# A Fourier mixing layer and a gated dense layer in seven-product blocks: the fifth block's second row taken from the first row's partial, and two blocks of dense columns by turns

## The chip, the cores and the metric

One core of one Trainium2 chip runs the whole kernel. The metric is the device time in microseconds (us) from the launch to the end, taken as the median of several executions. A profile of one further execution gives the times of single instructions.

## What is computed

`x` is 2048 tokens by 640 features. The result mixes a two-dimensional Fourier transform of `x` (real part) with a two-layer network, by a gate per token:

```python
a = x @ dft_hid_re.T                      # 2048 x 640
b = x @ dft_hid_im.T
fnet = dft_seq_re @ a - dft_seq_im @ b    # 2048 x 640, real part only
h = x @ w1 + b1                           # 2048 x 1728
dense = mish(h) @ w2                      # mish(h) = h * tanh(softplus(h))
g = sigmoid((x * gate_w).sum(-1))
out = g * fnet + (1 - g) * dense
```

## The kernel before

Four stages follow one another: `seq` (the transform along the 2048 tokens, real and imaginary part), `hid` (the transform along the 640 features), the dense first product with mish, and `out` (the dense second product, to which the gated Fourier part is added at the end). All numbers are float32. Each operand is split into a high and a low part (`split`: ScalarE copies with rounding, VectorE subtracts), and each product of blocks is three matmuls of 128x128 by 128x512 (`mm3`): high by high, high by low, low by high.

**Seven products.** `seq`, `hid` and `out` are written as problems (`sq[0..3]`, `hd[0..1]`, `ou[0..1]`). Each has five row blocks of 128 output features, of which four are computed as a two by two block product with seven instead of eight multiplications, and two column tiles `t1`, `t2` of 512. A problem has three parts. `first` runs the product with the block a11. `second` runs over the operands a22, a21, s2 and s1 (called "22", "21", "s2", "s1"). `third` runs "12", s3 and s4. The sums s1 = a21 + a22, s2 = s1 - a11, s3 = a11 - a21, s4 = a12 - a22 + s3 are formed by VectorE (`sums`) and split (`c_split`). Results grow in the eight accumulation banks, under the names `a`, `b`, `c`, `p4`, and `d1`, `d2` for the fifth row block, which is computed plainly: `d1` (column tile `t1`) gets a product with a11 in `first` and one with a12 in `third`; `d2` (tile `t2`) gets one with a22 and one with a21, both in `second`. `copy_out` copies banks to SBUF with ScalarE, `preload` copies SBUF values into a bank with ScalarE so that matmuls go on adding to them, `done` copies a finished bank out, `give` finishes the rows that s3 completes. In `ou[0]` `done` and `give` multiply by the gate and add the Fourier part, on VectorE. In `ou[1]` (`early`) the Fourier part is added to the partial values beforehand. Problems `sq[1]`, `sq[2]`, `hd[1]` and `ou[1]` run their `first` well ahead: its three banks are stored to DRAM (`aside`) and loaded again before `second`. `rest` adds to `out` the last 192 rows of the contraction.

**The dense first product** (`dense_first(tp)`, once for each half of the tokens) goes over six pairs of column blocks `fp`, with eight steps for each: p1, p5, d2, p6, p3, p7, p2, p4 (54 matmuls). Bank `a` is used by p1, then copied out by ScalarE (`snap`), added to by p6, copied out again, added to by p7, added to `KEEP["p5"]` by VectorE, and added to by p4. Bank `b` is used by p5, copied out, and added to by p3. So a step of the matmuls waits for a copy or an addition of an earlier step. `sums_of` (eight additions of VectorE) and `make` (splits of x) are attached to given steps by the lists at the end of the program.

**What sets the order.** The program is written out by hand, step by step. In the loop over steps, at step i: loads are issued up to `AHEAD` = 9 steps past those being prepared, when more SBUF slots (`FS`, 20) are free than `spare` reserves; the preparations of step i + 7 (6 in the dense stage) are issued; then the matmuls of step i; then stores that are due; then `post` of step i and the events `at(i, ...)`; then jobs (weights of a later stage: `low`, `top`, `w1`), as long as VectorE's planned clock is behind TensorE's. `store` queues a store three steps late. Each engine works its instructions in the order in which they are issued, and so does SyncE with nearly all loads and stores: a load of a scratch tensor waits there for the store of it, and a load into a slot for the last reader of the slot.

Of the kernel before, what the change touches and what calls it, by code (L numbers as in the profile page):

```python
# [13 lines left out]
P = 128  # L14
# [31 lines left out]
def fnet_mish_gate(ctx: ExitStack, tc: tile.TileContext, xn, xt, c_re, c_im, wd_re, wd_im,  # L46
# [134 lines left out]
    def b_sums(f, g):  # L181

        t = FS.get()
        tt(f[:, A2], f[:, B2], f[:, A2], OP.subtract)
        tt(f[:, B2], g[:, B2], f[:, B2], OP.subtract)
# [107 lines left out]
    class Problem:  # L293
# [8 lines left out]
        def first(self, new=False):  # L302
            st, kh = self.st, self.st.kh
            pa, pd = ("ax", "dx") if self.aside else ("a", "d1")
            for k in range(kh):
                key = ("c", st.kind, len(steps))
                raw = [(key, self.moving(self.t1, k))]
                start, last = not len(steps), k == kh - 1

                def prep(k=k, key=key):  # L310
                    if new:
                        f = RAW.pop(("xa", k))
                        top(st, k, f[:, A2], xd(k))
# [24 lines left out]
                if last:  # L338
                    takes[len(steps)] = 3 if self.aside else 2
                step(raw, [prep], mms, post if last else None)  # L340


        def second(self):
# [4 lines left out]
            def sums(k, raws):  # L348
                a22, a21, a11 = (RAW.pop(r[0]) for r in raws)
                s1 = FS.get()  # L350
                tt(s1, a21, a22, OP.add)
                tt(a11, s1, a11, OP.subtract)
                own.update({("22", k): a22, ("21", k): a21, ("s1", k): s1, ("s2", k): a11})
# [3 lines left out]
                "21": lambda k: [("d2", blocks(st.XA[k], 2 * P, 1))],  # L357
# [3 lines left out]
            opens = {("22", "p4"), ("22", "d2"), ("s1", "b")}  # L361
# [5 lines left out]
            def post(p, k):  # L367
# [4 lines left out]
                elif p == "21":  # L372
                    self.done("d2", 4, t2)
# [7 lines left out]
                    if self.aside:  # L381
                        d = [RAW.pop(("part", 2))]
                        if self.early:
                            y = YT.pop((4, t1))
                            tt(d[0], d[0], y, OP.add)
                            FS.put(y)
                        preload("d1", d)
                        FS.put(*d)
# [16 lines left out]
            if st.kind == "out":  # L405
# [4 lines left out]
                rest(t2, [("e", 2, True), ("e", 3, True), ("p4", 0, True), ("p4", 1, True), ("d2", 4, True)], e_post)  # L410
            for p, k in in_turn(kh, ("22", "21", "s2", "s1"), ("22", "21", "s2", "s1"), ("22", "21", "s2", "s1")):
# [7 lines left out]
                def mms(p=p, k=k, key=key):  # L419
# [4 lines left out]
                    if self.end and (p, k) in ends:  # L424
                        W.put(st.XA[k])
                        if k == kh - 1:
                            W.put(*[w for w in st.XT2 if w])
                preps.append(lambda p=p, k=k, key=key: c_split(key, own.pop((p, k))))
                step(raw, preps, mms, lambda p=p, k=k: post(p, k))
                if k == kh - 1:  # L430
                    takes[i] = (p == "21" or p == "s1" and 2) if self.early else 1 if p == "21" else 2
                    if self.early and p != "s1":
                        takes[i - 4] = 2
                        if p == "21":
                            self.y_load(i - 4, t2, 4)
                            self.y_load(i - 4, t1, 0, 1, 4)
                        else:
                            self.y_load(i - 4, *{"22": (t2, 0, 1), "s2": (t1, 2, 3)}[p])
                if (p, k) == ("21", kh - 1):
                    done = i  # L440
            if self.out:
                for t in (t1, t2):
                    at(n - 2, lambda t=t: QT.update({t: fs_load(qsc[t])}))
                self.y_load(done - 5, t2, 4)
            ends = {("s1", k) for k in range(kh)}
            if self.aside:
                for j in range(3):
                        at(n - 6 if j < 2 else done - 6, lambda j=j: RAW.update({("part", j): fs_load(self.aside[j])}))
# [3 lines left out]
        def third(self, over=False):  # L452
# [3 lines left out]
            def sums(k, raws):  # L456
                a12, a11, a21, a22 = (RAW.pop(r[0]) for r in raws)
                tt(a11, a11, a21, OP.subtract)
                FS.put(a21)
                tt(a22, a22, a11, OP.subtract)  # L460
                tt(a22, a12, a22, OP.subtract)
                own.update({("12", k): a12, ("s3", k): a11, ("s4", k): a22})
# [3 lines left out]
                "s3": lambda k: [("a", blocks(st.XT13[k], 2 * P, 2))],  # L466
# [13 lines left out]
            def post(p, k):  # L480
# [4 lines left out]
                elif p == "s3":  # L485
# [4 lines left out]
                    free_banks("a")  # L490
                elif p == "12":
# [5 lines left out]
            for p, k in in_turn(kh, ("12", "s3", "s4"), ("12", "s3", "s4"), ("s3", "12", "s4")):  # L497
# [14 lines left out]
                def mms(p=p, k=k, key=key):  # L512
# [4 lines left out]
                    op_done(key)  # L517
                    if self.end and p == "s4":
# [3 lines left out]
                if k == kh - 1 and p != "s3":  # L522
                    takes[i] = 3 if p == "12" else 2
                if self.out and k == kh - 1:
                    self.y_load(i - (4 if p == "s3" else 2), *{"s3": (t2, 0, 1, 2, 3), "12": (t1, 0, 1, 4), "s4": (t1, 2, 3)}[p])
# [5 lines left out]
        def done(self, name, d, t):  # L531

            for j, ps in enumerate(PS.pop(name)):
# [4 lines left out]
                elif self.early and name == "d2":  # L538
                    y = YT.pop((d, t))
                    tt(f, ps, y, OP.add)  # L540
                    FS.put(y)
# [192 lines left out]
    def dense_first(tp, end, ops):  # L734
# [32 lines left out]
        def sub(fp, ops, then=()):  # L767

            def mms():
                a, b, c = W1[fp]  # L770
                for bank, name, blk, start, stop in ops:
                    if start:
                        H[bank] = psum.get()
                    for k in range(2):
                        mm3(H[bank], *blk(a, b, c, k), *X[name, k, tp], start and k == 0, stop and k == 1)
                for bank, name, w, start, stop in then:
                    if start:
                        H[bank] = psum.get()
                    mm3(H[bank], *part((a, b)[w], 4 * P, 5 * P), *X[name, 0, tp], start, stop)
# [31 lines left out]
        for fp in range(FP):  # L811
            fa, fb = fp, fp + FP
            over = fp == FP - 1

            def free(*names, over=over):
# [3 lines left out]
            def p1_post(free=free):  # L819
                snap("p1", "a")  # L820
                free("a11")

            def p5_post(free=free):
                snap("p5", "b")
                free("s1")

            def p6_post(free=free):
                snap("u2", "a")
                free("s2")

            def p3_post(free=free, fb=fb):
                o = add("b", KEEP.pop("u2"))
                pop("b")
# [3 lines left out]
            def p7_post(free=free):  # L837
                add("a", KEEP["p5"])
                free("s3")

            def p2_post(free=free, fa=fa, fb=fb):
                c11, c22 = add("c", KEEP.pop("p1")), add("d", KEEP.pop("p5"))
                pop("c")
                pop("d")
# [5 lines left out]
            def p4_post(free=free, fa=fa, fp=fp):  # L850
                ps = H.pop("a")
# [10 lines left out]

            step([], [lambda fp=fp: need(("w1", fp))], sub(fp, [("a", "a11", at_cols(0, 0), True, True)]), p1_post)
            step([], [], sub(fp, [("b", "s1", at_cols(2, 0), True, True)]), p5_post)
            step([], [], sub(fp, [], [("d", "d2", 1, True, True)]))
            step([], [], sub(fp, [("a", "s2", t2_at(fp), False, True)]), p6_post)
            step([], [], sub(fp, [("b", "s4", at_cols(1, 2 * P), False, False)], [("b", "d1", 1, False, True)]), p3_post)
            step([], [], sub(fp, [("a", "s3", at_cols(2, 2 * P), False, True)]), p7_post)
            step([], [], sub(fp, [("c", "a12", at_cols(0, 2 * P), True, False)], [("c", "d1", 0, False, True)]), p2_post)
            step([], [], sub(fp, [("a", "a22", at_cols(1, 0), False, False)], [("a", "d2", 0, False, True)]), p4_post)  # L870
# [129 lines left out]
    for tp in range(2):  # L1000
# [132 lines left out]
```

## Time and profile before

| | |
|---|---|
| runs | 885.35, 886.82, 889.29 us (median 886.82) |
| profiled execution, first to last instruction (span) | 882.2 us |
| matmuls (TensorE) | 3780, busy 864.0 us (98% of the span) |
| VectorE | 1262 instructions, busy 724.2 us (82%) |
| ScalarE | 909 instructions, busy 477.5 us (54%) |
| DMA | 217.32 MB, 246 GB/s in the mean |

For the profiled execution only its span is given, 882.2 us; what lies around it is taken as the difference to the median of the runs, 4.6 us. In the profile's lines PE is TensorE, DVE is VectorE, ACT is ScalarE and SPq is SyncE's queue. Tile names are without buffer numbers: `ps` is a bank, `f` and `fx` are SBUF slots, `rh`, `rl` the high and low part of a moving operand, `wh`, `wl` those of a stationary one. "x3" at the end of a line counts instructions, and a bracket tells how long the engine had been idle and what ended that.

### The profile page before, as it was taken

What the parts mean: (1) busy time and instruction counts of PE and PEld (TensorE: products, weight loads), DVE (VectorE), ACT (ScalarE), POOL (GpSimd) and SP (SyncE); (2) the same over time, 40 slices, a digit from 0 to 9 for tenths busy, and PEclk for the clock granted to TensorE, in tenths of its full rate; (3) what the DMA queues carried; (4) which work ended last, traced back from release to release, by engine and by line L of the source; (5) the groups of instructions that cost most, each with busy time, mean ns of one, the idle gap of its engine ahead of it and who ended that gap; (6) DMA issues with size and microseconds to landing.
All of it is one profiled execution on the core that took longest, in us unless ns stands there. A gap on an engine that the chain in (4) does not pass through costs nothing.

```text
span 882.2 us, 12203 instructions
## 1 busy us (share of the span) xinstructions
PE 864.0 (98%) x3780; PEld 710.4 (81%) x3780; DVE 724.2 (82%) x1262; ACT 477.5 (54%) x909; POOL 0.2 (0%) x4
## 2 busy tenths in 40 slices
PE   8999999999999999999999999899899999999998
PEld 6888888888888888888888888687688788888886
DVE  5999987899799668998997987663875889798994
ACT  6756545454565545647665667543644656442442
POOL 0000000000000000000000000000000000000000
PEclk9999999999999999999999999999999999999999
DMA  9975759596889664768767795489676777394952
GB/s 323 328 236 175 245 185 324 164 312 235 302 275 351 202 221 156 259 226 283 265 236 273 247 316 178 138 308 367 204 256 214 268 260 240 133 330 142 367 203 107
DMA packets 119392, 217.32 MB, mean 246 GB/s; under 512 B 13600, under 2 KB 16032, under 8 KB 119328
## 3 DMA queue, kind: packets, MB, share of 16 engines
q1 hardware_dynamic: 119184, 216.43, 71.6%
q8 instruction: 29, 0.48, 0.2%
q14 instruction: 35, 0.29, 0.1%
q10 hardware_dynamic: 144, 0.13, 0.0%
HBM read 170.11 MB, written 46.40 MB: 245 GB/s over the span
## 4 chain that ended last, share of the span: by engine, by line
PE 93%; DVE 3%; ACT 1%; DMA 1%; issue 1%; SPq 0%; DVEq 0%; ACTq 0%
PE ps L89 93%; DVE f L77 1%; DVE wl L77 1%; ACT wh L80 1%; DMA y<-f 1%; DVE rl L77 0%; DMA f<-in_xn_dram 0%; ACT f L671 0%; DMA act<-f 0%; DVE fx L77 0%; ACT f L80 0%; ACT rh L80 0%; SPq L1031 0%; SPq L1051 0%; DVE f L477 0%
## 5 line engine op out<-in xcount | busy, mean ns | idle before, releaser
L89 PE MATMUL ps<-rh,wh 128*128 128x512 f32 x1067 | 415.7, 390 | 7.4 <-ACT f L80 3.4
L89 PE MATMUL ps<-rh,wl 128*128 128x512 f32 x1053 | 409.4, 389 | 0.0
L89 PE MATMUL ps<-rl,wh 128*128 128x512 f32 x1052 | 409.1, 389 | 0.0
L80 ACT ACTIVATE rh<-f 128x512 fp32r<-128x512 f32 x413 | 243.7, 624 | 158.3 <-DVE f L77 103.9
L77 DVE TENSOR_TENSOR rl<-f,rh 128x512 fp32r<-128x512 f32 x411 | 267.0, 685 | 47.7 <-ACT rh L80 47.0
L89 PEld LDWEIGHTS ps<-rh,wh 128*128 128x128 f32 x1067 | 200.4, 188 | 52.7 <-ACT f L80 5.0
L89 PEld LDWEIGHTS ps<-rh,wl 128*128 128x128 f32 x1053 | 197.7, 188 | 40.9
L89 PEld LDWEIGHTS ps<-rl,wh 128*128 128x128 f32 x1052 | 197.4, 188 | 40.9 <-DVE rl L77 0.2
L77 DVE TENSOR_TENSOR f<-f,f 128x512 f32<-128x512 f32 x303 | 207.0, 689 | 19.2 <-DMA u<-f 6.3
L80 ACT ACTIVATE f<-ps 128x512 f32<-128x512 f32 (+1 forms) x146 | 84.9, 593 | 92.7 <-PE ps L89 74.7
L80 ACT ACTIVATE wh<-f 128x512 fp32r<-128x512 f32 (+2 forms) x158 | 68.9, 475 | 49.4 <-DVE f L77 40.4
L77 DVE TENSOR_TENSOR f<-ps,f 128x512 f32<-128x512 f32 x90 | 59.0, 685 | 35.1 <-PE ps L89 35.1
L77 DVE TENSOR_TENSOR wl<-f,wh 128x512 fp32r<-128x512 f32 (+2 forms) x157 | 73.8, 502 | 16.2 <-ACT wh L80 16.0
L89 PE MATMUL ps<-wh,wh 128*128 128x512 f32 x201 | 79.3, 395 | 5.4 <-ACT f L80 2.8
L89 PE MATMUL ps<-wl,wh 128*128 128x512 f32 x196 | 77.0, 393 | 0.0
L89 PE MATMUL ps<-wh,wl 128*128 128x512 f32 x195 | 76.6, 393 | 0.0
L77 DVE TENSOR_TENSOR wl<-fx,wh 128x640 fp32r<-128x640 f32 (+3 forms) x82 | 43.7, 554 | 11.6 <-ACT wh L80 11.6
L671 ACT ACTIVATE f<-f,b1s 128x512 f32<-128x512 f32 x36 | 25.9, 721 | 49.2 <-DVE f L77 49.2
L89 PEld LDWEIGHTS ps<-wh,wh 128*128 128x128 f32 x201 | 38.0, 189 | 15.4 <-ACT f L80 4.2
L80 ACT ACTIVATE wh<-fx 128x128 fp32r<-128x128 f32 (+5 forms) x83 | 40.6, 514 | 10.5 <-DMA fx<-in_xn_dram 3.5
L89 PEld LDWEIGHTS ps<-wh,wl 128*128 128x128 f32 x195 | 37.0, 190 | 7.8
L89 PEld LDWEIGHTS ps<-wl,wh 128*128 128x128 f32 x196 | 37.1, 189 | 7.5
(43 smaller groups left out, 177.3 us busy)
## 6 DMA issues: line engine op xcount, KB each, us to landing
f<-in_c_re_dram SPq DMA_DIRECT2D x128, 256.0 KB, 4.2
f<-in_c_im_dram SPq DMA_DIRECT2D x128, 256.0 KB, 4.1
f<-act SPq DMA_DIRECT2D x84, 256.0 KB, 5.2
f<-u SPq DMA_DIRECT2D x80, 256.0 KB, 4.6
f<-in_xt_dram SPq DMA_DIRECT2D x64, 256.0 KB, 4.6
act<-f SPq DMA_DIRECT2D x54, 256.0 KB, 4.5
u<-f SPq DMA_DIRECT2D x40, 256.0 KB, 3.5
y<-f SPq DMA_DIRECT2D x40, 256.0 KB, 4.5
```

What stands on the lines that cost most here:

```text
L77: nc.vector.tensor_tensor(o, a, b, op=op)
L80: nc.scalar.activation(o, a, AF.Copy, scale=scale)
L89: nc.tensor.matmul(ps, a, b, start=start, stop=stop, skip_group_check=True)
L671: nc.scalar.activation(o[rows], src[rows], AF.Mish, bias=b1s[rows, f:f + 1])
```

## The change

**Fifth block.** With s3 taken as a21 - a11, the second column tile of the fifth row block is (five x a11) + (five x s3) + (its lower half x a22). So `d2` now begins as a copy of the partial value of `d1` after `first`; the "21" step of `second`, with its split of a21, goes; and "s3" of `third` gets one more product, into `d2`. Where `first` was run ahead, the partial is loaded six steps before `second`, and `preload` copies it into `d2`'s bank at the end of the step just before `second` (`d_ready`); in `ou[1]` VectorE first adds the Fourier part. `d2` is finished after s3, in `third`. It holds a bank from `first` or the beginning of `second` to there. The stationary blocks `XA` are given back in `third`. A problem has one step fewer for each k.

**Dense stage.** `dense_first` takes two pairs of column blocks by turns: p1 of the one, p1 of the other, p5 of the one, and so on. Banks have the names (a..d, 0) and (a..d, 1), eight in all. The lists that attach sums and splits to steps have new step numbers.

The counts in the built program: matmuls 3780 as before, VectorE's instructions 54 fewer, ScalarE's 41 fewer (54 splits gone; 8 preloads, 4 copies out and one copy more), the DMAs the same in number.

```diff
@@ Problem.first
                     else:
-                        KEEP["p1"] = copy_out("a", True)
+                        KEEP["p1"], KEEP["d"] = copy_out("a", True), copy_out("d1", True)
+                        preload("d2", KEEP["d"])
+                        FS.put(*KEEP.pop("d"))
@@ Problem.second
-                s1 = FS.get()
-                tt(s1, a21, a22, OP.add)
-                tt(a11, s1, a11, OP.subtract)
+                tt(a21, a21, a22, OP.add)
+                tt(a11, a21, a11, OP.subtract)
...
-                "21": lambda k: [("d2", blocks(st.XA[k], 2 * P, 1))],
...
+            def d_ready():
+                d = KEEP["d"] = RAW.pop(("part", 2))
+                if self.early:
+                    y = YT.pop((4, t2))
+                    tt(y, y, d, OP.add)
+                    preload("d2", [y])
+                    FS.put(y)
+                else:
+                    preload("d2", [d])
...
-            for p, k in in_turn(kh, ("22", "21", "s2", "s1"), ("22", "21", "s2", "s1"), ("22", "21", "s2", "s1")):
+            for p, k in in_turn(kh, ("22", "s2", "s1"), ("22", "s2", "s1"), ("22", "s2", "s1")):
...
+                at(n - 1, d_ready)
                 at(n, a_ready)
@@ Problem.third
-                tt(a11, a11, a21, OP.subtract)
-                FS.put(a21)
-                tt(a22, a22, a11, OP.subtract)
+                tt(a21, a21, a11, OP.subtract)
+                FS.put(a11)
+                tt(a22, a22, a21, OP.add)
...
-                "s3": lambda k: [("a", blocks(st.XT13[k], 2 * P, 2))],
+                "s3": lambda k: [("a", blocks(st.XT13[k], 2 * P, 2)), ("d2", blocks(st.XA[k], 2 * P, 1))],
...
                     free_banks("a")
+                    self.done("d2", 4, t2)
@@ dense_first
-        for fp in range(FP):
-            fa, fb = fp, fp + FP
+        def one(fp):
+            fa, fb, j = fp, fp + FP, fp % 2
...
+        for f0 in range(0, FP, 2):
+            for pair in zip(one(f0), one(f0 + 1)):
+                for st in pair:
+                    step(*st)
@@ program
-    dense_first(0, False, [("k0", n0 + 2), ("k1", n0 + 2), ("s1", n0 + 3), ("s2", n0 + 4), ("s4", n0 + 6), ("s3", n0 + 7)])
+    dense_first(0, False, [("k0", n0 + 2), ("k1", n0 + 2), ("s1", n0 + 3), ("s2", n0 + 6), ("s4", n0 + 8), ("s3", n0 + 10)])
     n0 = len(steps)
-    dense_first(1, True, [("a11", n0 - 1), ("k0", n0), ("k1", n0 + 1), ("s1", n0 + 1), ("d2", n0 + 2), ("s2", n0 + 3),
-                          ("s4", n0 + 4), ("d1", n0 + 4), ("s3", n0 + 5), ("a12", n0 + 6), ("a22", n0 + 7)])
+    dense_first(1, True, [("a11", n0 - 2), ("k0", n0 - 1), ("k1", n0), ("s1", n0 + 2), ("s2", n0 + 5), ("d2", n0 + 6),
+                          ("s4", n0 + 7), ("d1", n0 + 8), ("s3", n0 + 9), ("a12", n0 + 11), ("a22", n0 + 13)])
```

More of the change, by code (lines that the diff above doesn't have):

```diff
@@ L338, in first @@
                 if last:
-                    takes[len(steps)] = 3 if self.aside else 2
+                    takes[len(steps)] = 3
                 step(raw, [prep], mms, post if last else None)
@@ L381, in post @@
                     if self.aside:
-                        d = [RAW.pop(("part", 2))]
+                        d = KEEP.pop("d")
                         if self.early:
                             y = YT.pop((4, t1))
-                            tt(d[0], d[0], y, OP.add)
+                            tt(d, d, y, OP.add)
                             FS.put(y)
-                        preload("d1", d)
-                        FS.put(*d)
+                        preload("d1", [d])
+                        FS.put(d)
                 elif p == "s2":
@@ L409, in second @@
                     self.y_load(n - 4, t2, 2, 3)
-                rest(t2, [("e", 2, True), ("e", 3, True), ("p4", 0, True), ("p4", 1, True), ("d2", 4, True)], e_post)
-            for p, k in in_turn(kh, ("22", "21", "s2", "s1"), ("22", "21", "s2", "s1"), ("22", "21", "s2", "s1")):
+                rest(t2, [("e", 2, True), ("e", 3, True), ("p4", 0, True), ("p4", 1, True), ("d2", 4, False)], e_post)
+            for p, k in in_turn(kh, ("22", "s2", "s1"), ("22", "s2", "s1"), ("22", "s2", "s1")):
                 i, key = len(steps), ("c", st.kind, len(steps))
@@ L423, in mms @@
                     op_done(key)
[L424 to L427, printed above, removed]
+                    if self.end and p == "s2" and k == kh - 1:
+                        W.put(*[w for w in st.XT2 if w])
                 preps.append(lambda p=p, k=k, key=key: c_split(key, own.pop((p, k))))
@@ L430, in second @@
                 if k == kh - 1:
-                    takes[i] = (p == "21" or p == "s1" and 2) if self.early else 1 if p == "21" else 2
+                    takes[i] = (p == "s1" and 2) if self.early else 2
                     if self.early and p != "s1":
                         takes[i - 4] = 2
-                        if p == "21":
-                            self.y_load(i - 4, t2, 4)
+                        if p == "22":
+                            self.y_load(i - 4, t2, 0, 1)
                             self.y_load(i - 4, t1, 0, 1, 4)
                         else:
-                            self.y_load(i - 4, *{"22": (t2, 0, 1), "s2": (t1, 2, 3)}[p])
-                if (p, k) == ("21", kh - 1):
-                    done = i
+                            self.y_load(i - 4, t1, 2, 3)
             if self.out:
@@ L443, in second @@
                     at(n - 2, lambda t=t: QT.update({t: fs_load(qsc[t])}))
-                self.y_load(done - 5, t2, 4)
-            ends = {("s1", k) for k in range(kh)}
             if self.aside:
                 for j in range(3):
-                        at(n - 6 if j < 2 else done - 6, lambda j=j: RAW.update({("part", j): fs_load(self.aside[j])}))
+                    at(n - 6, lambda j=j: RAW.update({("part", j): fs_load(self.aside[j])}))
+                if self.early:
+                    self.y_load(n - 6, t2, 4)
+                at(n - 1, d_ready)
                 at(n, a_ready)
@@ L517, in mms @@
                     op_done(key)
+                    if self.end and p == "s3":
+                        W.put(st.XA[k])
                     if self.end and p == "s4":
@@ L521, in third @@
                 step(raw, preps, mms, lambda p=p, k=k: post(p, k))
-                if k == kh - 1 and p != "s3":
-                    takes[i] = 3 if p == "12" else 2
+                if k == kh - 1:
+                    takes[i] = {"12": 3, "s3": 1, "s4": 2}[p]
                 if self.out and k == kh - 1:
-                    self.y_load(i - (4 if p == "s3" else 2), *{"s3": (t2, 0, 1, 2, 3), "12": (t1, 0, 1, 4), "s4": (t1, 2, 3)}[p])
+                    self.y_load(i - (4 if p == "s3" else 2), *{"s3": (t2, 0, 1, 2, 3, 4), "12": (t1, 0, 1, 4), "s4": (t1, 2, 3)}[p])
                     if p == "s4":
@@ L537, in done @@
                     self.add_y(d + j, t, f)
[L538 to L541, printed above, removed]
                 else:
@@ L772, in mms @@
                     if start:
-                        H[bank] = psum.get()
+                        H[bank, fp % 2] = psum.get()
                     for k in range(2):
-                        mm3(H[bank], *blk(a, b, c, k), *X[name, k, tp], start and k == 0, stop and k == 1)
+                        mm3(H[bank, fp % 2], *blk(a, b, c, k), *X[name, k, tp], start and k == 0, stop and k == 1)
                 for bank, name, w, start, stop in then:
                     if start:
-                        H[bank] = psum.get()
-                    mm3(H[bank], *part((a, b)[w], 4 * P, 5 * P), *X[name, 0, tp], start, stop)
+                        H[bank, fp % 2] = psum.get()
+                    mm3(H[bank, fp % 2], *part((a, b)[w], 4 * P, 5 * P), *X[name, 0, tp], start, stop)
             return mms
@@ L848, in p2_post, with p4_post @@
                 free("a12", "d1")
-            def p4_post(free=free, fa=fa, fp=fp):
-                ps = H.pop("a")
+            def p4_post():
+                ps = H.pop(("a", j))
                 def last():
@@ L861, in p4_post @@
                         W.put(T2B[fp // KD])
[L863 to L870, printed above, removed]
+            return [
+                ([], [lambda: need(("w1", fp))], sub(fp, [("a", "a11", at_cols(0, 0), True, True)]), p1_post),
+                ([], [], sub(fp, [("b", "s1", at_cols(2, 0), True, True)]), p5_post),
+                ([], [], sub(fp, [], [("d", "d2", 1, True, True)])),
+                ([], [], sub(fp, [("a", "s2", t2_at(fp), False, True)]), p6_post),
+                ([], [], sub(fp, [("b", "s4", at_cols(1, 2 * P), False, False)], [("b", "d1", 1, False, True)]), p3_post),
+                ([], [], sub(fp, [("a", "s3", at_cols(2, 2 * P), False, True)]), p7_post),
+                ([], [], sub(fp, [("c", "a12", at_cols(0, 2 * P), True, False)], [("c", "d1", 0, False, True)]), p2_post),
+                ([], [], sub(fp, [("a", "a22", at_cols(1, 0), False, False)], [("a", "d2", 0, False, True)]), p4_post),
+            ]
+        for f0 in range(0, FP, 2):
+            for pair in zip(one(f0), one(f0 + 1)):
+                for st in pair:
+                    step(*st)
         for name, i in ops:
```

42 lines of the change are left out of this document (20 added, 22 removed).

## The prediction

> **What bounds the kernel now.** I read the page first, then the windows of busy time, the waits, the chain in order of time, and last the timeline around the places that the change touches. The page:
>
> ```profile
> span 882.2 us, 12203 instructions
> PE 864.0 (98%) x3780; PEld 710.4 (81%) x3780; DVE 724.2 (82%) x1262; ACT 477.5 (54%) x909; POOL 0.2 (0%) x4
> ...
> PE 93%; DVE 3%; ACT 1%; DMA 1%; issue 1%; SPq 0%; DVEq 0%; ACTq 0%
> ```
>
> TensorE is busy for 98% of the span and carries 93% of the chain. The windows (PE, PEld, DVE, ACT and POOL busy with counts, then granted clock, DMA share, GB/s) say where the rest lies. The second is the dense stage, the fourth a part of it:
>
> ```profile
> 7.40:554.50 547.10, 547.10 (x2413) 453.02 (x2414) 472.36 (x818) 320.14 (x608) 0.00 (x0) 1.00 0.74 252
> 554.50:706.30 151.80, 140.96 (x604) 112.97 (x603) 103.97 (x197) 76.70 (x151) 0.00 (x0) 0.99 0.75 256
> 706.30:878.40 172.10, 172.10 (x757) 141.89 (x757) 146.18 (x243) 77.88 (x146) 0.00 (x0) 1.00 0.65 224
> ...
> 620.00:640.00 20.00, 16.37 (x64) 12.64 (x63) 15.98 (x27) 11.86 (x22) 0.00 (x0) 0.91 0.56 187
> ```
>
> In `seq`, `hid` and `out` TensorE is never idle: one matmul starts each 547.10 / 2413 = 0.2267 us, and in `out` each 172.10 / 757 = 0.2273. Nothing can be won there without fewer matmuls, and their number stays 3780. The dense stage has 604 matmuls, worth 604 x 0.2267 = 136.9 us, and lasts 151.8. So **14.9 us** is all that any reordering can win. The waits of TensorE's weight loads (total, count, longest) and the timeline show of what these 14.9 are made:
>
> ```profile
> PEld ps L89 <- ACT f L80: 9.2, 10, 2.8
> PEld ps L89 <- DVE f L77: 6.3, 4, 1.8
> ```
> ```profile
> 620.82 0.39 PE L89 MATMUL ps<-rh,wl 128*128 128x512 f32 x1
> 623.61 0.58 PE L89 MATMUL ps<-wh,wh 128*128 128x512 f32 x1 [2.39 <-ACT f L80]
> 623.98 0.63 PE L89 MATMUL ps<-wl,wh 128*128 128x512 f32 x1
> ...
> 627.36 0.40 PE L89 MATMUL ps<-rh,wh 128*128 128x512 f32 x1
> ```
>
> They are the waits of a step for the copy out of its bank, or for the addition into it. After the wait of 2.39 us matmuls come (627.36 - 623.61) / 9 = 0.42 us apart, and the granted clock of that window is 0.91. So a wait of that size costs 627.36 - 623.61 - 9 x 0.2267 = **1.7 us** more, as long as TensorE runs slowly behind it. The Trainium skill, "TensorE: Matmul & The Clock Gate", section "What's actually happening", has TensorE at half rate after an idle window of some 3.4 us. This trace does not agree on the length: 2.39 us idle were enough. By the page the wait of 3.2 us that I leave in the dense stage below would be free of this price, and the sum 1.7 lower.
>
> **Fewer splits: nothing.** The 54 splits that go are these two rows:
>
> ```profile
> L77 DVE TENSOR_TENSOR rl<-f,rh 128x512 fp32r<-128x512 f32 x411 | 267.0, 685 | 47.7 <-ACT rh L80 47.0
> L80 ACT ACTIVATE rh<-f 128x512 fp32r<-128x512 f32 x413 | 243.7, 624 | 158.3 <-DVE f L77 103.9
> L80 ACT ACTIVATE f<-ps 128x512 f32<-128x512 f32 (+1 forms) x146 | 84.9, 593 | 92.7 <-PE ps L89 74.7
> ```
>
> VectorE loses 54 x 0.685 = 37 us, ScalarE net some 41 x 0.6 = 25 us. All of it lies in windows one and three, behind matmuls that never wait. Worth 0. The price of the edit is in what its new copies must wait for.
>
> **Dense stage: -9.5.** In the trace two dependent steps (p1 and p6, p5 and p3, p6 and p7) have one short step of 9 matmuls or so between them: 9 x 0.2267 = 2.0 us. With two pairs by turns there are about 24, 5.4 us. The worst lag before was 2.0 + 2.6 = 4.6 us (start of 620.82 to 623.61 is 2.79, less one spacing), below 5.4, so nearly all waits go. One stays: in the last pairs of the first half the additions of `sums_of` for the second half stand on VectorE just ahead of p7's addition.
>
> ```profile
> 619.06 5.40 DVE L77 TENSOR_TENSOR f<-f,f 128x512 f32<-128x512 f32 x8
> ```
>
> Eight sums 5.4, two splits 1.3 and three additions 1.9 make 8.6 us, against 5.4 of cover: a wait of 3.2, with the clock's 1.7, and 0.5 for small ones: 5.4 left of 14.9. Bounds of the gain: 4.6 (a second such wait) to 12.9 (2.0 left, when half of the sums are done in idle time before). The eight banks being all taken costs nothing here, since no other problem runs in this stage.
>
> **Fifth block, start of `sq[1]`: +2.6.** `d2` now needs a preload by ScalarE just before `second`. In the changed program's order ScalarE has ahead of it the split of the first "22" pair, two steps on, and the two copies of bank `b`. Before, the split stood behind.
>
> ```profile
> f<-in_c_im_dram SPq DMA_DIRECT2D x128, 256.0 KB, 4.1
> ```
> ```profile
> 131.56 2.19 SPq L1060 DMA_DIRECT2D u<-f  x4
> 134.04 1.41 SPq L1051 DMA_DIRECT2D f<-in_c_im_dram  x3
> ...
> 137.64 1.28 ACT L80 ACTIVATE f<-ps 128x512 f32<-128x512 f32 x2 [0.40 <-PE ps L89]
> 139.48 0.39 PE L89 MATMUL ps<-rh,wh 128*128 128x512 f32 x1
> ```
>
> The load for that split is issued behind the four stores and three loads of these rows, at 135.45. It lands 4.1 later, at 139.5; split 0.6, two copies 1.3, preload 0.6: 142.1. The first matmul into `d2` is the one at 139.48. So 2.6 us. Bounds: 1.3 (the load one place earlier or landing as quickly as the fast ones) and 4.3 (with the clock's 1.7; the wait is just of the size of the one that brought it). At the starts of `sq[2]`, `sq[3]` and `hd[1]` the loads stand earlier: 0.2 together.
>
> **Gates: +1.2.** With `d2` holding a bank through `third`, the gate sums of problems 1 and 3 find all eight banks taken and wait for the copy of a finished one, 0.593 us each time. Bounds 0.7 and 2.
>
> **`out`, first crossing: +10.5.** `ou[0]` has `d2` in a bank from its beginning, so when its `rest` starts after `ou[1].first`, its second bank must be one of `ou[1].first`'s, to be freed by ScalarE's copies. Before they were these, and ended in time:
>
> ```profile
> 733.35 1.55 ACT L80 ACTIVATE f<-ps 128x512 f32<-128x512 f32 x3
> ```
>
> That matmul is number 3145 of 3780, wanted at 706.30 + (3145 - 3023) x 0.2273 = 734.0. In the changed program ScalarE has ahead of the copies the splits of the first "21" and s1 operands for `ou[0].second`, and these wait for loads by SyncE. Before:
>
> ```profile
> 697.85 0.32 SPq L1060 DMA_DIRECT2D act<-f  x1
> 701.78 0.32 SPq L1051 DMA_DIRECT2D f<-act  x1
> ...
> 712.30 0.42 SPq L1060 DMA_DIRECT2D act<-f  x1
> ...
> 716.08 0.80 SPq L1051 DMA_DIRECT2D f<-act  x2
> ...
> 720.72 2.91 SPq L1051 DMA_DIRECT2D f<-act  x4
> ```
>
> Twice a load waits for the store of the same block, 3.9 and 3.8 us, and all loads behind it wait too. In the changed order the first such store stands behind matmul 3071, wanted at 717.2 (the store at 712.30 stood behind matmul 3054, 713.3, and ran 1.0 ahead of it; I allow up to 4.5, so 712.7 to 717.2); the second follows at once. Then 13 more transfers until the last load that the splits need, at (720.72 - 716.08) / 9 = 0.52 each. Together 3.9 + 0.9 + 3.8 + 6.8 = 15.4: issued at 728.1 to 732.6. Before, from the same load (second of the four at 720.72, some 0.6 later) to the copies it took 733.35 - 721.3 = 12.0, and a copy is 0.6. So the copy ends at 740.7 to 745.2, in the middle 742.9, and TensorE waits 742.9 - 734.0, **8.8** with rounding, and 1.7 for the clock. Bounds 6 (part of the 12.0 was waiting, too) to 11.
>
> **`out`, second crossing: +9.0.** At the start of `ou[1].second` VectorE adds the Fourier part to the partial and ScalarE preloads the sum; the matmul that needs it is number 3480, wanted at 706.30 + 457 x 0.2273 = 810.2. VectorE then has in its queue the whole end of `ou[0]`, which is gated and added there:
>
> ```profile
> 798.20 0.69 DVE L77 TENSOR_TENSOR f<-ps,f 128x512 f32<-128x512 f32 x1 [3.02 <-PE ps L89]
> ...
> 814.86 0.69 DVE L77 TENSOR_TENSOR f<-f,f 128x512 f32<-128x512 f32 x1
> ```
> ```profile
> 811.00 0.60 ACT L80 ACTIVATE ps<-fx 128x512 f32<-128x512 f32 x1 [12.79 <-DVE f L77]
> ```
>
> These are 26 instructions back to back, 798.20 to 815.55 = 17.35 us. In the changed order 28 stand ahead of the new addition, since `d2` is finished there too. The first starts 3 matmuls earlier, at 797.5. So 797.5 + 17.35 + 2 x 0.67 + 0.69 = 816.9, preload 0.60: 817.5, against 810.2: a wait of 7.3, and 1.7. Before, this queue cost TensorE nothing: the preload at 811.00, behind the additions up to there, held up no matmul. Bounds 5.9 and 8.0 (two instructions less, one more).
>
> **At nothing:** ScalarE's other preloads and copies of `d2` (0.6 each, beside matmuls that go on into other banks; ScalarE is busy 54%); the later return of `XA` (the w1 weights that take its place are split in jobs that still end before `hid` does; without that cover the dense stage would begin late by a split or two, 1.3 each); the moved loads of the partials (same number of DMAs, but they pass SyncE's queue six steps before `second`, where each is one more issue of some 0.5 us); sums in place (same duration, one buffer less).
>
> **Sum.** -9.5 + 2.6 + 0.2 + 1.2 + 10.5 + 9.0 = **+14.0**: span 882.2 + 14.0 = 896.2. The runs' median 886.82 is 4.6 above the span, so **900.8**. All low ends: -12.9 + 1.3 + 0.2 + 0.7 + 7.7 + 7.6 = +4.6, 891; all high ends: -4.6 + 4.3 + 0.2 + 2 + 12.7 + 9.7 = +24.3, 911.
>
> **The rivals.** *Faster: VectorE and ScalarE run ahead (0.12).* With 37 and 25 us less to do, they reach the crossings of `out` early enough, so that the copies and the addition are done before they are wanted. Then 10.5 and 9.0 go: +14.0 - 19.5 = -5.5, 881.3; with the dense stage wholly cleared 876. It decides as soon as VectorE reaches the end of `ou[0]` 7.3 us earlier. For it: VectorE is busy 82%, the most loaded after TensorE. Against it: at 798.20 it had been idle 3.02 us for TensorE, and at 811.00 ScalarE had been idle 12.79 for VectorE; a lighter queue does not start earlier, where its first instruction waits for a matmul.
>
> *Only one of the two crossings waits (0.14).* The first may go if SyncE runs still further ahead, as VectorE's lighter work frees its slots earlier: +3.5, 890.3. Or the second, if the sum is worked before the gate's additions: +5.0, 891.8.
>
> *The dense stage does not do what it says (0.10).* Additions of both pairs meet on VectorE, so that each window has twice the work in twice the time, and the lag stays as long as the cover. VectorE is busy 103.97 of 151.80 us there, which speaks against it. Then -9.5 is nearer 0: +23.5, 910.3. Longer crossings than I count give the same.
>
> **How the numbers follow.** The forecast has 0.64. The range 889 to 910 takes it and the one-crossing case; outside are the faster case (0.12) and half of the last (0.05). About 0.5% (4.4 us) is what a measurement can tell from no change: 882.4 to 891.3 counts as same. Faster: 0.12. Same: half of the one-crossing case and a little of the forecast's low end, 0.09. Slower: 0.79.
>
> **What would show it.** In the profile after: TensorE's idle time in the dense stage falls from 14.9 to some 5, with one wait on an addition by VectorE; a wait on ScalarE's preload near 139.5 us; one on ScalarE's copy ahead of `ou[0].second`; one on the preload after VectorE's additions at matmul 3480; and granted clock under 1.00 just behind each. It is wrong if the window of `out` still shows TensorE idle for nothing, or if the dense stage keeps more than 10 us.

## The result, and the profile after

| | before | changed |
|---|---|---|
| median of four runs | 887.87 us | 900.19 us |
| lowest to highest | 885.35 to 889.29 | 897.25 to 902.07 |
| span of the profiled execution | 882.2 us | 898.5 us |

The ratio is 1.0141, with a 95% interval of 1.0116 to 1.0167: slower by 1.4%. The forecast was 900.8 us, with a range of 889 to 910. The sum came out; one of its two largest terms stood for the wrong reason, as the experiments show, and two other errors offset each other.

The page of the changed kernel, first its span, the busy times and the chain:

```profile
span 898.5 us, 12032 instructions
PE 869.0 (97%) x3780; PEld 714.1 (79%) x3780; DVE 693.6 (77%) x1208; ACT 457.7 (51%) x868; POOL 0.2 (0%) x4
...
PE 87%; DVE 5%; DMA 4%; issue 2%; ACT 1%; SPq 1%; DVEq 0%; ACTq 0%
```

VectorE is busy 31 us less (724.2 to 693.6) and ScalarE 20 (477.5 to 457.7), and the kernel is slower. TensorE's matmuls are as many, its share of the chain fell from 93% to 87%. The windows of busy time, cut at nearly the same matmuls as in the prediction (start of the dense pairs, start of `out`), with two short ones behind the longest waits:

```profile
7.58:561.67 554.09, 550.40 (x2413) 453.53 (x2414) 450.71 (x780) 305.39 (x580) 0.00 (x0) 1.00 0.72 248
561.67:703.48 141.81, 138.59 (x603) 114.00 (x602) 90.87 (x168) 68.44 (x133) 0.00 (x0) 0.99 0.76 260
703.48:894.60 191.12, 176.16 (x758) 144.04 (x756) 150.25 (x257) 81.00 (x153) 0.00 (x0) 0.96 0.63 213
739.00:743.00 4.00, 3.56 (x8) 2.84 (x9) 3.84 (x10) 3.85 (x8) 0.00 (x0) 0.50 0.92 295
824.00:828.50 4.50, 3.86 (x9) 3.06 (x10) 3.70 (x7) 3.81 (x7) 0.00 (x0) 0.52 1.03 366
```

The dense stage is 10.0 us shorter (151.80 to 141.81), `seq` and `hid` are 7.0 longer (547.10 to 554.09), and `out` 19.0 (172.10 to 191.12). Behind the two long waits of `out` the granted clock is 0.50 and 0.52. TensorE's waits, total, count, longest, and the first matmul behind each of the four large ones:

```profile
PEld ps L89 <- ACT ps L80: 10.2, 6, 6.2
PEld ps L89 <- ACT f L80: 8.9, 2, 8.6
PEld ps L89 <- DVE f L77: 7.7, 5, 3.6
```
```profile
143.28 0.50 PE L89 MATMUL ps<-rh,wh 128*128 128x512 f32 x1 [1.84 <-ACT ps L80]
...
626.24 0.50 PE L89 MATMUL ps<-rh,wh 128*128 128x512 f32 x1 [3.23 <-DVE f L77]
...
739.44 0.80 PE L89 MATMUL ps<-rh,wh 128*128 128x512 f32 x1 [8.15 <-ACT f L80]
...
824.64 0.79 PE L89 MATMUL ps<-wh,wh 128*128 128x512 f32 x1 [5.72 <-ACT ps L80]
```

They are the four that the prediction placed: the preload of `d2` in `sq[1]`, p7's addition, the copies ahead of `ou[0]`'s `rest` (matmul 3145), and the preload of `ou[1]` (matmul 3480).

To compare kernels I use one figure for each stretch: the sum, over its matmuls, of the distance from the start before less 0.2267 us. That is what TensorE lost there, waiting or slowed. Stretches go by matmul number, counted from 0: start (to 100), `seq` and `hid` (to 2284), dense (to 3032), first crossing of `out` (to 3300), second (to 3600), rest. All ten profiled executions, with the medians of the runs, in us:

| kernel | median | start | seq, hid | dense | 1st crossing | 2nd crossing | rest |
|---|---|---|---|---|---|---|---|
| before | 887.87 | 4.2 | -0.1 | 15.4 | 0.0 | 0.0 | 0.3 |
| changed | 900.19 | 6.0 | 5.3 | 5.3 | 10.1 | 9.3 | 0.0 |
| E1 dense part only | 887.14 | 6.6 | -0.1 | 4.1 | 10.3 | 0.0 | 0.0 |
| E2 fifth block only | 901.86 | 6.0 | 6.8 | 13.7 | 0.5 | 10.1 | 0.0 |
| E3 changed, Fourier part added late | 895.28 | 6.3 | 5.1 | 4.7 | 10.1 | 2.4 | 4.1 |
| E4 changed, copies first | 899.70 | 7.1 | 5.3 | 5.2 | 8.2 | 10.1 | 0.0 |
| E5 dense part, w2 loads held | 877.49 | 4.1 | -0.1 | 6.4 | 0.1 | 0.4 | 1.1 |
| E6 as E5, sums later | 873.80 | 7.4 | -0.1 | 1.6 | 0.3 | 0.5 | 0.2 |
| E7 changed, w2 loads held | 891.64 | 6.2 | 5.3 | 4.0 | 3.7 | 9.4 | 0.0 |
| E8 changed, three edits | 885.24 | 6.3 | 5.0 | 5.0 | 2.4 | 1.7 | 2.8 |

The start differs from execution to execution by up to 3 us with the same code in it, so single profiles are compared by the other columns.

### The profile page after: what moved, and what is told of

It reads as the page before. It is cut to its first block, busy times and chain, and to the rows that moved or that the text cites. A ratio compares the mean times of both kernels' runs of the same rounds, so it can differ in the third digit from the quotient of the medians.

```text
span 898.5 us, 12032 instructions
## 1 busy us (share of the span) xinstructions
PE 869.0 (97%) x3780; PEld 714.1 (79%) x3780; DVE 693.6 (77%) x1208; ACT 457.7 (51%) x868; POOL 0.2 (0%) x4
## 4 chain that ended last, share of the span: by engine, by line
PE 87%; DVE 5%; DMA 4%; issue 2%; ACT 1%; SPq 1%; DVEq 0%; ACTq 0%
PE ps L89 87%; DVE f L77 3%; DMA act<-f 1%; DVE rl L77 1%; DMA f<-act 1%; DMA f<-in_xt_dram 0%; DMA f<-in_xn_dram 0%; SPq L1062 0%; DVE wl L77 0%; SPq L1071 0%; ACT f L80 0%; DMA f<-in_c_re_dram 0%; DMA f<-in_c_im_dram 0%; ACT rh L80 0%; ACT wh L80 0%
## 5 line engine op out<-in xcount | busy, mean ns | idle before, releaser
L89 PE MATMUL ps<-rl,wh 128*128 128x512 f32 x1036 | 404.6, 391 | 0.0
L80 ACT ACTIVATE rh<-f 128x512 fp32r<-128x512 f32 x370 | 221.2, 625 | 175.8 <-DVE f L77 108.3
L77 DVE TENSOR_TENSOR rl<-f,rh 128x512 fp32r<-128x512 f32 x367 | 242.2, 686 | 78.2 <-ACT rh L80 77.4
L77 DVE TENSOR_TENSOR f<-f,f 128x512 f32<-128x512 f32 x314 | 214.7, 689 | 24.5 <-DMA f<-act 5.6
L89 PE MATMUL ps<-wh,wh 128*128 128x512 f32 x212 | 83.2, 393 | 6.8 <-ACT ps L80 5.7
L89 PE MATMUL ps<-wl,wh 128*128 128x512 f32 x212 | 82.7, 390 | 0.0
L89 PE MATMUL ps<-wh,wl 128*128 128x512 f32 x207 | 80.8, 390 | 0.0
L77 DVE TENSOR_TENSOR f<-ps,f 128x512 f32<-128x512 f32 x86 | 56.0, 684 | 31.0 <-PE ps L89 31.0
L77 DVE TENSOR_TENSOR wl<-fx,wh 128x640 fp32r<-128x640 f32 (+3 forms) x78 | 40.7, 547 | 9.2 <-ACT wh L80 9.2
L80 ACT ACTIVATE wh<-fx 128x128 fp32r<-128x128 f32 (+5 forms) x79 | 37.7, 506 | 5.3 <-DMA fx<-in_xn_dram 3.5
```

The costliest lines, as they stand in the source:

```text
L77: nc.vector.tensor_tensor(o, a, b, op=op)
L80: nc.scalar.activation(o, a, AF.Copy, scale=scale)
L89: nc.tensor.matmul(ps, a, b, start=start, stop=stop, skip_group_check=True)
```

## The experiments

The theory on record was additive: the dense part wins about 10 us, the fifth block costs about 24, of it 10 at each crossing of `out`. E1 and E2 do one part alone. Ratios are against runs of the kernel before on the same chip, with medians of 886.87 us for E1 to E4 and 886.67 for E5 to E8 (887.87 beside the changed kernel). Kernels with different medians of the kernel before are compared by these ratios.

**E1, the dense part alone.** `dense_first` by turns and its two lists; all of the fifth block as before.

```diff
+        for f0 in range(0, FP, 2):
+            for pair in zip(one(f0), one(f0 + 1)):
+                for st in pair:
+                    step(*st)
```

> Only the dense stage by turns; the fifth block as before. If the terms of the sum stand alone: the dense stage loses some 5.2 us of matmul starts instead of 15.0, the rest never waits, so about 877 us, -9.7 against before. Rival: the two parts of the change depend on each other (the later stores of the activations by turns hold up the loads of the out stage whatever the fifth block does): then a wait of 3 to 10 us stands in the out stage and the time is 880 to 887 us.

Measured: 887.14 us, ratio 1.0000 (0.9986 to 1.0015). The rival was right. The dense column falls from 15.4 to 4.1, and 10.3 come back at the first crossing, without any change in the fifth block. The matmul that waits, and SyncE's queue ahead of it:

```profile
733.77 0.80 PE L89 MATMUL ps<-rh,wh 128*128 128x512 f32 x1 [7.30 <-ACT f L80]
```
```profile
695.87 0.46 SPq L140 DMA_DIRECT2D f<-in_w_dram  x1
706.36 0.33 SPq L135 DMA_DIRECT2D fx<-in_w_dram  x1
706.74 0.42 SPq L140 DMA_DIRECT2D f<-in_w_dram  x1
707.21 0.42 SPq L1067 DMA_DIRECT2D act<-f  x1
711.00 0.33 SPq L1058 DMA_DIRECT2D f<-act  x1
711.37 0.91 SPq L1067 DMA_DIRECT2D act<-f  x2
715.08 0.80 SPq L1058 DMA_DIRECT2D f<-act  x2
```

```profile
SPq L135 <- DVE wl L77: 9.9, 1, 9.9
```

From 696.3 to 706.4 SyncE issues nothing: a load of the weights w2 (L135) waits for its buffer, whose last reader is a split on VectorE. The store of act block 4 (act: the output of mish, the operand of `out`) stands behind it, its load waits 3.8 us for that store, then the same once more for block 5. By turns, blocks 4 and 5 are finished together at the end of the stage, so their stores come behind this w2 load; in the kernel before, the store of block 4 went at 697.85, ahead of it.

**E2, the fifth block alone.** The hunks of `Problem`; the dense stage as before.

```diff
-            for p, k in in_turn(kh, ("22", "21", "s2", "s1"), ("22", "21", "s2", "s1"), ("22", "21", "s2", "s1")):
+            for p, k in in_turn(kh, ("22", "s2", "s1"), ("22", "s2", "s1"), ("22", "s2", "s1")):
+                at(n - 1, d_ready)
```

> Only the fifth block; the dense stage as before. If the crossings of the out stage come from the fifth block alone: 887 + 10.1 (bank for e) + 9.3 (second d2) + 5.1 (preloads and gates in seq) = about 911 us. Rival: the first crossing is long because the loads for it wait for activations that by turns are stored late; with the old dense order they come 4 to 8 us earlier, the first crossing shrinks to 0 to 5 us and the time is 901 to 906 us.

Measured: 901.86 us, ratio 1.0188 (1.0160 to 1.0216), at the rival's lower end. The first crossing is down to 0.5, though `d2` keeps its bank in `ou[0]` here as in the changed kernel. The second stays, 10.1:

```profile
825.03 0.80 PE L89 MATMUL ps<-rh,wh 128*128 128x512 f32 x1 [5.71 <-ACT ps L80]
```

So the fifth block alone costs 15 us, the dense part alone nothing, and the loss at the first crossing comes with the dense part.

**E3, the second crossing.** The changed kernel, but `ou[1]`'s `d2` is preloaded with the bare partial, and the Fourier part is added by VectorE when the bank is finished.

```diff
@@ d_ready
-                if self.early:
-                    y = YT.pop((4, t2))
-                    tt(y, y, d, OP.add)
-                    preload("d2", [y])
-                    FS.put(y)
-                else:
-                    preload("d2", [d])
+                preload("d2", [d])
@@ done
+                elif self.early and name == "d2":
+                    y = YT.pop((d, t))
+                    tt(f, ps, y, OP.add)
+                    FS.put(y)
```

> The changed kernel, but the second column tile's Fourier part is added to d2 when it is finished (in third), not to the partial before the preload; the preload then waits for ScalarE alone. If the wait at matmul 3480 (5.9 us, 1.6 behind it) is VectorE's queue, it goes, and the time is 900 - 7.5 = about 893 us. Rival: the step would wait for p4's bank or the next operands anyway (a wait of 1.25 us stands at matmul 3470 already): 896 to 899 us.

Measured: 895.28 us, ratio 1.0101 (1.0069 to 1.0133), between the two; by the ratios that is 3.5 us less than the changed kernel. The wait at matmul 3480 is gone and the second crossing falls from 9.3 to 2.4, which shows that VectorE's queue made the wait. But a new one stands 30 us behind (matmul 3611), at the preloads of `c` and `d1`, which take their Fourier part from VectorE too:

```profile
851.15 0.50 PE L89 MATMUL ps<-rh,wh 128*128 128x512 f32 x1 [2.22 <-ACT ps L80]
```
```profile
850.49 1.81 ACT L80 ACTIVATE ps<-f 128x512 f32<-128x512 f32 x3 [10.59 <-DVE f L77]
```

TensorE reaches matmul 3611 7.4 us sooner than in the changed kernel (it could start it at 848.77 instead of 856.21), VectorE hardly: the preloads start at 850.49 instead of 851.61.

**E4, the copies ahead in ScalarE's queue.** In the changed kernel no splits beyond the first step of `ou[0].second` are issued until the copies are, and no weight jobs.

```diff
+    hold.update({i: n + 1 for i in range(n - 7, n)})
...
-        while ready < n_all and ready <= i + (LEAD_D if ready in narrow else LEAD):
+        while ready < n_all and ready <= min(i + (LEAD_D if ready in narrow else LEAD), hold.get(i, n_all)):
```

> The changed kernel, but for the last seven steps before the rest of the first out problem no splits beyond that problem's first step are issued and no weight jobs in five of them, so that the copies out of ou[1].first's banks stand ahead on ScalarE. If the wait at matmul 3145 (8.3 us, 1.8 behind it) comes from the copies' place in the queue, it goes and the time is about 890 us. Rival: the operands themselves come late (their loads stand behind two loads that wait for stores), and the wait only moves to the steps of 22 right behind: 896 to 900 us.

Measured: 899.70 us, ratio 1.0145 (1.0126 to 1.0165), the rival's time. The wait at matmul 3145 is gone, and four others stand 20 to 32 us behind it; the first crossing still loses 8.2. The last and costliest three:

```profile
758.91 0.50 PE L89 MATMUL ps<-rl,wh 128*128 128x512 f32 x1 [1.63 <-DVE rl L77]
762.39 0.50 PE L89 MATMUL ps<-rh,wh 128*128 128x512 f32 x1 [1.37 <-ACT rh L80]
764.52 0.80 PE L89 MATMUL ps<-rl,wh 128*128 128x512 f32 x1 [1.63 <-DVE rl L77]
```

They wait for splits. So the place of the copies in the queue is where the lateness shows, not where it comes from. That late loads are its source, as the rival has it, E4 does not show by itself, since its edit also issues these splits later; E5 tests the loads.

**E5, the w2 loads held back.** E1's kernel, with no loads for weight jobs issued in seven steps, from one ahead of the first step of `ou[0].first` on.

```diff
-        while jobs and ... and i >= 2:
+        while jobs and ... and i >= 2 and i - n_dense not in range(-1, 6):
```

> Dense stage by turns with the fifth block as before, and the loads of w2 for the jobs of the out stage not issued from one step ahead of ou[0].first to six steps on, so that the stores and loads of act blocks 4 and 5 do not stand behind a w2 load on SyncE (which waited from 696.3 to 706.4 us for its buffer in the kernel with the dense part alone). If that is the cause of the wait of 7.5 us at ou[0]'s rest: the copies come 7 to 10 us earlier, the wait goes and the time is about 878 us. Rival: the two loads that wait for their own stores (3.8 us each) carry it: 2 to 4 us of it stay, 881 to 884 us.

Measured: 877.49 us, ratio 0.9896 (0.9879 to 0.9912), as expected. The wait is gone (0.1 instead of 10.3), with the two loads still waiting for their stores:

```profile
700.87 0.33 SPq L1067 DMA_DIRECT2D act<-f  x1
702.93 0.33 SPq L1058 DMA_DIRECT2D f<-act  x1
703.35 0.86 SPq L1067 DMA_DIRECT2D act<-f  x2
707.41 0.80 SPq L1058 DMA_DIRECT2D f<-act  x2
```

TensorE is ready for matmul 3150 at the same time in both kernels (726.2 and 726.3), so their times can be compared. The store of block 4 goes at 700.87 instead of 707.21, its load at 702.93 instead of 711.00. ScalarE's copies, the upper line from E1, the lower from E5, start 7.6 us sooner, which is more than the 7.30 that TensorE waited in E1:

```profile
733.14 1.55 ACT L80 ACTIVATE f<-ps 128x512 f32<-128x512 f32 x3
```
```profile
725.54 1.55 ACT L80 ACTIVATE f<-ps 128x512 f32<-128x512 f32 x3
```

So the loss at the first crossing comes from the weight loads in SyncE's queue. The edit holds all of them for seven steps; that it is the one with the wait of 9.9 us follows from its place in the queue and its size, and was not tried by itself.

**E6, the last wait of the dense stage.** As E5, and the eight sums for the second half of the tokens are attached behind p7's additions.

```diff
-... ("k0", n0 - 1), ("k1", n0), ("s1", n0 + 2) ...
+... ("k0", n0 + 2), ("k1", n0 + 2), ("s1", n0 + 2) ...
```

> As the kernel with the w2 loads held back, and in addition the eight sums for the second half of the tokens issued two and three steps later, behind p7's two additions. If those sums ahead of the addition make the dense stage's last wait (2.6 to 3.4 us, 1.6 behind it): it goes, 4 to 5 us less than the run before it, about 873 us. Rival: the splits of s1 and s2 then come late and p5 waits as long: the same 878 us.

Measured: 873.80 us, ratio 0.9850 (0.9833 to 0.9867), as expected, and the fastest of all, 1.5% under the kernel before. The dense column falls from 6.4 to 1.6. Its dense stage and `out`, cut at the same matmuls:

```profile
557.70:695.79 138.09, 137.56 (x603) 112.68 (x602) 92.23 (x172) 69.24 (x136) 0.00 (x0) 1.00 0.78 266
695.79:868.20 172.41, 172.38 (x758) 141.54 (x756) 156.83 (x269) 84.05 (x161) 0.00 (x0) 1.00 0.70 236
```

**E7, the same held loads in the changed kernel.** The edit of E5 alone.

> The changed kernel with the w2 loads held back in the same way. If the first crossing in it has the same cause as with the dense part alone, its wait of 8.3 us and 1.8 behind it go: about 890 us. Rival: the fifth block keeps a bank more, so that the copies, though earlier, still come too late: 893 to 897 us.

Measured: 891.64 us, ratio 1.0052 (1.0032 to 1.0073), between the two. By the ratios some 8 us go, 6.4 of them at the first crossing. That keeps 3.7, a wait of 2.0 and the slow clock behind it.

```profile
732.08 0.56 PE L89 MATMUL ps<-rh,wh 128*128 128x512 f32 x1 [1.84 <-ACT f L80]
```

This is the share of the bank that `d2` holds: here matmul 3145 needs the copies, in E1 matmul 3150 did, five matmuls or 1.1 us later. The other 0.9 is the copy itself: it starts 1.4 us after TensorE is ready for matmul 3145, in E5 0.5 after. Why, I did not take apart.

**E8, three edits on the changed kernel.** E7, with E3's late addition, and in `seq` the split of the step n + 6 is issued behind `d2`'s preload:

```diff
+                if st.kind == "seq":
+                    hold[n - 1] = n + 5
```

> The changed kernel with the w2 loads held back, the Fourier part of d2 added when it is finished, and in seq the split that stood ahead of d2's preload issued one step later. If the terms add up: 900 - 10 - 5 (as measured for the late addition) - 2.1 = about 883 us, so still no better than the dense part with the w2 loads held back. Rival: with the first crossing gone the other waits in third come earlier and are as long: 886 to 890 us.

Measured: 885.24 us, ratio 0.9990 (0.9972 to 1.0009), between the two. In `sq[1]` ScalarE's preload now starts at 140.93 instead of 142.63, but a wait of 1.43 us at 146.02 takes the place of the one of 1.84 at 143.28, so that `seq` and `hid` lose 5.0 instead of 5.3. The wait behind the second crossing is there too (2.8 in the last column). With these three edits the changed fifth block is still 7.8 us behind E5, and 11.4 behind E6. E8 has the wait of the dense stage that E6 removes (5.0 in its column), and some of the other waits only moved.

## Why the prediction was right, and where it was not

**The bound** was right: in `seq`, `hid` and `out` TensorE never waited, so 54 splits fewer on VectorE and ScalarE won nothing. E2 removes them all and is 15 us slower.

**Dense stage**, forecast -9.5: measured 15.4 to 5.3, -10.1. Its remaining wait was forecast with 3.2 us and measured with 3.23, for the stated reason: two lots of four sums stand around one addition and ahead of p7's, and E6, which moves them, removes it. That the hundredths agree is luck: in the other kernels that have it, this wait was 2.17 (E7) to 3.22 us (E4). VectorE's timeline in the changed kernel:

```profile
619.60 2.74 DVE L77 TENSOR_TENSOR f<-f,f 128x512 f32<-128x512 f32 x4
622.25 0.68 DVE L77 TENSOR_TENSOR f<-ps,f 128x512 f32<-128x512 f32 x1
622.85 2.73 DVE L77 TENSOR_TENSOR f<-f,f 128x512 f32<-128x512 f32 x4
625.50 1.28 DVE L77 TENSOR_TENSOR f<-ps,f 128x512 f32<-128x512 f32 x2
```

**Start of `sq[1]`**, forecast +2.6: 1.84 idle, 2.0 from start to start, in the order of ScalarE's queue that was given: split, which waited for its load, two copies, preload.

```profile
141.14 0.63 ACT L80 ACTIVATE rh<-f 128x512 fp32r<-128x512 f32 x1 [2.62 <-DMA f<-in_c_im_dram]
141.67 1.07 ACT L80 ACTIVATE f<-ps 128x512 f32<-128x512 f32 x2
142.63 0.60 ACT L80 ACTIVATE ps<-f 128x512 f32<-128x512 f32 x1
```

**Gates and the other starts**, forecast 1.2 and 0.2: the two gate sums cost 0.97 each, and the banks are given back by VectorE's additions, not by a ScalarE copy as the price was taken from; the other starts cost 1.2. Both terms were too small, together by 1.7.

**Second crossing**, forecast +9.0: 9.3, and the step holds line by line. VectorE's first addition, the last two before the preload, and the preload itself:

```profile
804.67 0.69 DVE L77 TENSOR_TENSOR f<-ps,f 128x512 f32<-128x512 f32 x1 [6.43 <-PE ps L89]
...
822.65 1.29 DVE L77 TENSOR_TENSOR f<-f,f 128x512 f32<-128x512 f32 x2
```
```profile
823.98 0.60 ACT L80 ACTIVATE ps<-f 128x512 f32<-128x512 f32 x1 [21.34 <-DVE f L77]
```

From 804.67 to 823.94 VectorE works 29 instructions without a pause, the last of which is the new addition. 19.3 us; forecast were 19.4. Of the wait, 1.25 us had gone already to another one ten matmuls ahead (matmul 3470, on the bank for `p4`).

**First crossing**, forecast +10.5: 10.1 in size, and the wrong cause. The step that failed is "`ou[0]` has `d2` in a bank from its beginning, so ... its second bank must be one of `ou[1].first`'s". E2 has that bank held and loses 0.5; E1 has it free and loses 10.3. The half of the step on SyncE was right, that stores and loads of act blocks stand later in the changed order and wait twice for each other, but I took that order as given, and did not ask which part of the change made it. It was the dense part. Nor did I see the w2 load whose buffer holds up the first store. In the changed kernel:

```profile
701.84 0.45 SPq L140 DMA_DIRECT2D f<-in_w_dram  x1
712.32 0.33 SPq L135 DMA_DIRECT2D fx<-in_w_dram  x1
712.70 0.42 SPq L140 DMA_DIRECT2D f<-in_w_dram  x1
713.17 0.42 SPq L1071 DMA_DIRECT2D act<-f  x1
716.94 0.33 SPq L1062 DMA_DIRECT2D f<-act  x1
```

The bracket of 712.7 to 717.2 for that store held 713.17, also on the scale of the kernel before, where TensorE is ready for matmul 3145 2.9 us later (716.1). But in E7, without the w2 load ahead of it, the same store goes at 705.92, 709.9 on that scale and ahead of the bracket:

```profile
705.92 0.33 SPq L1071 DMA_DIRECT2D act<-f  x1
```

So it was the load that I did not see that put the store into the bracket, and the size of this term is luck. The forecast for the whole change came out, but its working would have given -9.5 for the dense part alone, where 0 was measured, and some +23 for the fifth block alone, where 15 was measured.

**From span to median.** I added 4.6 us for what lies around the span. The runs' own figures show 1.8 us (900.28 for a span of 898.5). The profiled execution of before had a quick start (4.2 in the table, 6.0 in the changed kernel), which the 4.6 held as well. The span grew by 16.3, of which 1.8 is this start; the medians by 12.3. So the forecast of the span, 896.2, was 2.3 too low and the 4.6 was 2.8 too high; that the two offset each other, which left the median 0.6 us off, is luck.

**Rivals.** That a lighter VectorE runs ahead did not happen: at 804.67 it had been idle 6.43 us for TensorE. That the dense order would not help in its stage was wrong, too; that only one crossing waits fits neither.

## What to carry to other kernels

When TensorE is never idle in a stage, work taken off other engines there wins nothing, and each new operand that must be ready at a boundary is a price. When an order by turns makes two results finish together, look at what their stores and reloads now stand behind in the one queue that does the transfers: a reordering that wins 10 us in its stage can give them back in the next, and holding back an unrelated load returned them. Cost each part of a change with the other part undone, or a sum can be right with its terms in the wrong place.

## What the runs showed of the hardware

A wait of TensorE slows the clock behind it, but not by its length alone. The lengths here are start to start, less 0.23 us, and the wait after the warm-up at the very start is left out. Single waits up to 1.91 us (E4) left the spacing at 0.23 us. All of 3.28 us and more were followed by six to twelve matmuls 0.43 us apart, with 1.7 to 2.9 us lost. In between it went either way. At matmul 590, 2.00 us did not bring it in the changed kernel, and 2.03 us did in E2 (1.7 lost). Elsewhere, 2.56 us brought it in the kernel before, 2.55 in E1 and 2.99 in E2 did not. The prediction put a price of 1.7 us on its three waits of 3.2 us and more, and for the one of 2.6 only into the bounds; one row had stood for it. The Trainium skill, "TensorE: Matmul & The Clock Gate", section "What's actually happening", describes a window of some 3.4 us that runs freely, so that the moment of a change depends on where in the window it falls, and half rate after an idle window. That it goes either way between 2 and 3 us agrees with that; that 3.4 us of idle time are needed does not: 2.0 us were enough in E2 and E7.
